# Decode attention and FFN on one core: joint operations for the last three tokens, some paired K loads, and a new order of the work

## The chip, the core and the metric

The kernel runs on one core of a Trainium2 chip. The metric is the device time in microseconds (us) of one execution; before the change its median is 295.55 us in 3 runs (294.45 to 295.8). The engines are PE (matrix multiply; PEld is its weight load), DVE (vector), ACT (scalar functions), POOL (GpSimd) and SP, which here only issues loads and stores to the 16 DMA engines.

## What is computed

Two layers, each an attention step on a cached window and a SwiGLU FFN, for one new position of four sequences (called tokens here):

```python
x = x + A(layernorm(x));  x = x + B(layernorm(x))      # layer 0
x = x + A(layernorm(x));  x = x + B(layernorm(x))      # layer 1: same weights, same caches
# A: B=4, Sq=1, D=448, 16 query heads, 8 K/V heads, Dh=256, window of the last 2048 positions
q = x @ wq; p = softmax(q @ k.T * Dh**-0.5); o = p @ v; return o @ wo
# B: F=1792
return (silu(x @ w_gate) * (x @ w_up)) @ w_down
```

All data are bf16 in memory. One K or V of a token and a head is 1 MB (2048 x 256), and there are 32 of each.

## The kernel before

**Pairs.** The unit of work is a pair of a token and a K/V head in one layer; there are 2 x 32. K and V come in halves of 512 KB, in a pool of 27 slots `half`. For five of the eight heads (`KEEP_K`, `KEEP_V`) the turned K and the V stay in the pool from layer 0 to layer 1, so 44 pairs are loaded and 20 are not. A pair runs through: loads (L852, L872); a DVE turn of each K half into another slot (L858); POOL spreads the query (L875); PE scores, 16 matmuls for each half (L885, with L889); maximum and mask on DVE and PE (L899 to L910); exp on ACT (L913); fold and weights (L918, L921); sums (L927, L930); PV in two halves, either with 512 columns moving (L950) or with V as weights (L943, the last pairs). Then the result is scaled (POOL power L978 or DVE reciprocal L975, L982 to L1001) and projected with `wo` (L1015), accumulated in PSUM bank A. PE gives a K slot back after the scores and a V slot after PV, and SP waits for that before it issues a load into the slot.

**Tokens.** When the eight heads of a token in a layer are done come residual (L740), norm (L560 to L609: sums on DVE, totals over partitions on PE L579, subtraction L583, spread L586, variance L591 to L593, power on POOL L605), FFN (gate and up L693, tanh on ACT L706, products L709 to L717, down L729) and, after layer 0, the next norm and the q projection in three parts (L639 to L661) of two, two and four heads. Pairs of token t-1 in layer 1 alternate with pairs of token t in layer 0. Token 0 is stored on its way; tokens 1 to 3 end together: residual and norm for each (with the two multipliers L608 and L609 on POOL), then one FFN for three in two halves of the columns, written as rows with the residual added through an identity (L761, L777), copied (L784) and stored (L786).

**What sets the order.** The program lists all operations with their dependences, an estimated duration and a rank: the pair's position plus an offset for its kind in three phases (`RANK`) plus a correction for single operations (`TWEAK`). `schedule` walks through time with these estimates and lets each engine take the ready operation of lowest rank; the result is a fixed instruction order for each engine, SP among them. It also hands out the pool's slots: a load takes the slot that has been free longest while more than `RESERVE` are free, and turns use one more spare slot. On the chip each engine runs its list in order and waits on semaphores.

Of the kernel before, what the change touches and what calls it, by code (L numbers as in the profile page):

```python
# [13 lines left out]
B = 4  # L14
# [35 lines left out]
STAY = 0.3  # L50
PAT = 4
ENTER = 0
# [9 lines left out]
RESERVE = 1  # L62
ISSUE = 0.45
LAND = 0.9
DSTART = 2.7
PAGE, PAGE0 = 128, 85
FETCH = 2.65
BUMP = 1.3
# [12 lines left out]
    "exp": (1, 1, 3),  # L81
    "flip": (2, -2, 1.5),
    "fold": (-1, -3, -1.5),
    "high": (-3, -3, -3),
    "inv": (0.6, -0.3, 0),
    "load_k": (0.6, 0, -0.3),
    "load_v": (-0.6, 0, 1),
    "low": (3, -0.3, 1.5),
    "mask": (0, -1, -0.3),
    "max": (0.6, 1, -0.6),  # L90
    "most": (-1, -1.5, 0),
    "neg": (0.3, -0.6, 0),
    "proj": (-1.5, 3, 0.6),
    "pv": (0.3, 1, 0),
    "q": (2, -1.5, -1.5),
    "q_last": (2, 2, 2),
    "scale": (-1.5, 1, -1),
    "scores": (-1, 1.5, 3),
    "spread": (-1, -1, -1),
    "sum": (0.3, -1.5, 3),  # L100
    "sums": (-3, -2, 0),
    "turn": (0.6, 3, -1.5),
    "turn_s": (-3, -3, -3),
    "weights": (2, 1, 1.5),
# [34 lines left out]
class Op:  # L139
# [3 lines left out]
    def __init__(self, i, eng, dur, rank, emit):  # L143
        self.i, self.eng, self.dur, self.rank, self.emit = i, eng, dur, rank, emit
        self.deps = {}
        self.succ = []
        self.nbytes = 0
        self.dsem = None
        self.dval = 0
        self.cell = None  # L150
        self.rel = ()
        self.swap = None
        self.mm = 0
        self.drain = 0.0
        self.inc = False
        self.val = 0
        self.waits = []


class Graph:  # L160
# [56 lines left out]
    def schedule(self, npool):  # L217
# [22 lines left out]
        while n < len(self.ops):  # L240
            best = None
            for e, lst in avail.items():
                if not lst:
                    continue
# [891 lines left out]
```

## Time and profile before

| | |
|---|---|
| median of the runs | 295.55 us |
| the profiled execution | 293.74 us |
| its span, first to last instruction | 291.6 us |
| read from HBM | 104.44 MB |
| share of the span busy: PE, DVE, POOL, ACT | 77%, 74%, 21%, 20% |
| K halves, V halves loaded | 88, 88, of 512 KB |

Times are from the span's start. A row of a group has line, engine, operation, output<-inputs, shapes and xcount, then busy us and mean ns of one. A row of the waits has who waited, for whom, and the total us, number and longest. A row of instructions in time has start, us, engine, line. A stretch of the span has start:end, length, busy us and count of PE, PEld, DVE, ACT and POOL, the granted clock of PE, the DMA engines' busy share and GB/s.

### The profile page before, as it was taken

To read this page: it belongs to the slowest core of one execution; us is meant where nothing else is said; L and a number is where in the kernel's file an instruction comes from. 1 tells how busy PE (TensorE), PEld (TensorE's weight loads), DVE (VectorE), ACT (ScalarE), POOL (GpSimd) and SP (SyncE) were. 2 spreads that over 40 slices of the span, in tenths; PEclk is the share of its full clock that TensorE was granted. 3 is DMA by queue.
4 is the path that set the end of the run, shared out by engine and by line. 5 is a ranking of instruction groups with operands and counts; after the bars stand their busy time and mean duration, and the time that the engine had idled before them with its cause. 6 is when DMAs were issued, how large, how long until landed. Compare 5 with 4: busy or idle time off the path is not lost.

```text
span 291.6 us, 11945 instructions
## 1 busy us (share of the span) xinstructions
PE 223.2 (77%) x5262; PEld 158.1 (54%) x5262; DVE 216.8 (74%) x759; ACT 57.5 (20%) x173; POOL 62.2 (21%) x137
## 2 busy tenths in 40 slices
PE   0544665556649998878896998697989879899984
PEld 0432433334528654656673645574855559675873
DVE  8597556666328979988767988875988997769762
ACT  1002112211001231221112322121123120033311
POOL 1312111111102322221220522022132211142130
PEclk9999999999999999999999999999996555555555
DMA  6999999999999999999999999999899999999400
GB/s 265 393 401 406 405 403 403 402 404 405 387 410 388 405 407 406 410 375 376 398 340 405 410 406 407 364 376 374 297 390 416 407 405 329 290 353 406 198 2 3
DMA packets 31076, 105.20 MB, mean 361 GB/s; under 512 B 3117, under 2 KB 7218, under 8 KB 30642
## 3 DMA queue, kind: packets, MB, share of 16 engines
q1 hardware_dynamic: 31018, 104.45, 92.9%
q8 instruction: 41, 0.67, 0.9%
q14 instruction: 9, 0.07, 0.1%
q10 hardware_dynamic: 8, 0.00, 0.0%
HBM read 104.44 MB, written 0.00 MB: 358 GB/s over the span
## 4 chain that ended last, share of the span: by engine, by line
PE 40%; DMA 27%; DVE 14%; SPq 12%; issue 4%; ACT 1%; POOL 1%; DVEq 0%
DMA half<-in_A_k_cache_dram 24%; PE S L885 11%; PE Y L950 11%; DVE half L858 8%; SPq L872 6%; SPq L852 4%; PE A L1015 3%; PE Z L693 3%; PE Z L639 3%; DMA half<-in_A_v_cache_dram 3%; SPq L537 2%; PE Z L729 2%; PE S L902 2%; PE S L889 2%; PE Y L943 1%
## 5 line engine op out<-in xcount | busy, mean ns | idle before, releaser
L858 DVE STREAM_TRANSPOSE half<-half 128x1024 uint32<-128x1024 uint32 x88 | 108.4, 1232 | 9.5 <-DMA half<-in_A_k_cache_dram 8.8
L885 PE MATMUL S<-qe,half 128*128 128x8 bf16 x2048 | 71.2, 169 | 24.0 <-DVE half L858 14.0
L885 PEld LDWEIGHTS S<-qe,half 128*128 128x128 bf16 x2048 | 64.6, 105 | 33.6 <-DVE half L858 19.1
L950 PE MATMUL Y<-half,pT 128*16 128x512 bf16 x440 | 58.5, 602 | 2.0 <-DMA half<-in_A_v_cache_dram 0.8
L913 ACT ACTIVATE praw<-S,small 128x128 bf16<-128x128 f32 x64 | 23.5, 368 | 136.8 <-DVE S L907 117.0
L978 POOL TENSOR_TENSOR small<-small,expo 128x4 f32<-128x4 f32 (+1 forms) x33 | 29.9, 907 | 65.8 <-DVE small L930 59.8
L875 POOL TENSOR_TENSOR qe<-qc,qmask 128x64 bf16<-128x64 bf16 x64 | 18.7, 292 | 99.6 <-PE S L889 64.7
L982 ACT ACTIVATE oha<-Y 128x512 bf16<-128x512 f32 x33 | 19.6, 595 | 30.0 <-PE Y L950 29.8
L984 DVE SCALAR_TENSOR_TENSOR oha<-oha,small,Y 128x512 bf16<-128x512 bf16 x33 | 24.0, 727 | 1.5 <-ACT oha L982 1.4
L1015 PE MATMUL A<-oT,wo_sb 128*128 128x1 bf16 (+1 forms) x640 | 23.5, 167 | 1.7 <-DVE oT L1001 1.4
L1015 PEld LDWEIGHTS A<-oT,wo_sb 128*128 128x128 bf16 x640 | 21.8, 106 | 4.0 <-DVE oT L1001 2.3
L921 ACT ACTIVATE pT<-S 128x64 bf16<-128x64 f32 x64 | 14.3, 223 | 40.6 <-PE S L918 40.5
L905 DVE STREAM_TRANSPOSE S<-S 128x32 f32<-128x32 f32 x64 | 13.8, 217 | 10.6 <-PE S L902 10.0
L899 DVE TRANSPOSE_TENSOR_REDUCE pmax<-S 128x1 bf16<-128x32 f32 x64 | 13.4, 210 | 11.0 <-PE S L889 8.8
L605 POOL TENSOR_TENSOR st<-st,expo 128x1 f32<-128x1 f32 x16 | 9.0, 561 | 55.7 <-DVE st L593 46.5
L902 PE MATMUL S<-identb,pmax 128*128 128x128 bf16 x64 | 17.8, 278 | 1.6 <-DVE pmax L899 1.4
L907 DVE TENSOR_TENSOR S<-S,amask 128x128 f32<-128x128 f32 x64 | 18.4, 291 | 0.1
L639 PE MATMUL Z<-xn,wq_sb 128*128 128x1 bf16 (+1 forms) x480 | 15.2, 166 | 3.1 <-issue 2.7
L639 PEld LDWEIGHTS Z<-xn,wq_sb 128*128 128x128 bf16 x480 | 14.1, 104 | 5.9 <-issue 2.8
L889 PE MATMUL S<-pbig,identb 128*128 128x128 bf16 x64 | 17.1, 267 | 0.0
L910 DVE TENSOR_REDUCE small<-S 128x1 f32<-128x128 f32 x64 | 16.5, 259 | 0.0
L950 PEld LDWEIGHTS Y<-half,pT 128*16 128x16 bf16 x440 | 8.8, 91 | 13.2 <-DMA half<-in_A_v_cache_dram 5.6
(124 smaller groups left out, 232.4 us busy)
## 6 DMA issues: line engine op xcount, KB each, us to landing
half<-in_A_k_cache_dram SPq DMA_DIRECT2D x88, 512.0 KB, 8.2
half<-in_A_v_cache_dram SPq DMA_DIRECT2D x88, 512.0 KB, 7.7
wo_sb<-in_A_wo_dram SPq DMA_DIRECT2D x8, 448.0 KB, 14.4
wq_sb<-in_A_wq_dram SPq DMA_DIRECT2D x3, 1024.0 KB, 6.9
wd_sb<-in_B_w_down_dram SPq DMA_DIRECT2D x1, 1568.0 KB, 16.6
wg_sb<-in_B_w_gate_dram SPq DMA_DIRECT2D x1, 1344.0 KB, 17.5
wu_sb<-in_B_w_up_dram SPq DMA_DIRECT2D x1, 1344.0 KB, 16.0
wq_sb<-in_A_wq_dram SPq DMA_DIRECT2D x1, 512.0 KB, 10.4
```

The source lines that it names most:

```text
L639: last = e.matmul(o, lhsT=cols(cc, h, ee), rhs=rhs, start=(cc == 0 and hh == 0 and ee == 0), stop=(cc == 3), skip_group_check=True)
L858: return e.transpose(dst[:, :, k0:k1, :], src[:, :, k0:k1, :])
L875: g.op(POOL, 0.25, rk("spread", pos - SLEAD - 1), lambda e: e.tensor_tensor(qe[q_][:, :, :, :], qc[t][:, kvh, :, :].unsqueeze(2).broadcast ...
L885: last = e.matmul(Sb[s_][:, 16 * hf + 8 * gg:16 * hf + 8 * gg + 8], lhsT=kt[:, gg, ce // 2, ce % 2, :], rhs=qe[q_][:, ce, :, :], start=(hf ...
L889: last = e.matmul(Sb[s_][:, 128:256], lhsT=identb[:, :], rhs=pbig[:, :].unsqueeze(1).broadcast_to([128, 64, 2]), start=True, stop=False, s ...
L902: g.op(PE, 0.06, rk("most", pos), lambda e: e.matmul(Sb[s_][:, 128:256], lhsT=pmax[s_][:, 0:1].broadcast_to([128, 128]), rhs=identb[:, :], ...
L913: g.op(SCA, 0.28, rk("exp", pos), lambda e: e.activation(praw[pos % NP][:, :], sM[s_][:, :, :].rearrange("p a r -> p (a r)"), ACT.Exp, bia ...
L950: last = e.matmul(Yb[p_][32 * gg:32 * gg + 16, :], lhsT=pT[mi][:, u:u + 2, :, :, :].rearrange("p u m y n -> p (u m y n)"), rhs=half[vs[hv] ...
L978: g.op(POOL, 0.4 + 0.27 * nm, rk("inv", pos), lambda e: e.tensor_tensor(ri[r_][:, 0:2 * nm], rs[r_][:, 0:2 * nm], expo[:, 1:1 + 2 * nm], o ...
L982: g.op(SCA, 0.48, rk("high", pos), lambda e: e.activation(oh[p_][:, :], Yb[p_][:, :], ACT.Copy), r=(f"y{p_}",), w=(f"oh{p_}",), bank=by)
L984: g.op(DVE, 0.63, rk("low", pos), lambda e: e.scalar_tensor_tensor(out=oh[p_][:, :], in0=oh[p_][:, :], scalar=lomask[:, 0:1], in1=Yb[p_][: ...
L1015: last = e.matmul(Av[:, cc, sl], lhsT=wo_sb[:, 4 * kvh + k, c0:c0 + 128], rhs=oT[ok][:, k % 2, k // 2, 0:n], start=False, stop=False, skip ...
```

## The change

*Last three tokens.* `residuals` and `norms` do for tokens 1 to 3 together, after the last projection, what `residual` and `norm` did for each; the sums are a product and a reduction in place of one operation with an accumulator. One power on POOL serves all three, and the multipliers 0.5r and 0.5r^2 of it are gone: in the FFN of these tokens gate and up are first multiplied by r (the power) on DVE, then one tanh with an immediate scale and two products follow for each half.

```diff
+        def norms(ts, rank, z):
...
+            vec(rank, lambda e: e.tensor_tensor(S_[:, :, 2:6], X, wrow[:, :].unsqueeze(1).broadcast_to([128, n, 4]), op=ALU.mult),
+            vec(rank, lambda e: e.tensor_reduce(S_[:, :, 0:1], S_[:, :, 2:6], AX.X, ALU.add), kw, kv, 0.09)
+            vec(rank, lambda e: e.tensor_tensor(S_[:, :, 2:6], S_[:, :, 2:6], X, op=ALU.mult), kx + kw, kw, 0.08)
+            vec(rank, lambda e: e.tensor_reduce(S_[:, :, 1:2], S_[:, :, 2:6], AX.X, ALU.add), kw, kv, 0.09)
...
+            g.op(POOL, 0.4 + 0.135 * n, rank, lambda e: e.tensor_tensor(
+                S_[:, :, 8:9], S_[:, :, 9:10], expo[:, 0:1].unsqueeze(1).broadcast_to([128, n, 1]), op=ALU.pow), r=kh + ("expo",), w=kr)
...
+                if rows:
...
+                    vec(rank, lambda e, js=js, zg=zg, of=of: e.tensor_tensor(sub(gsf, js), sub(zg[:, 0:gw], js), of(8), op=ALU.mult),
+                    g.op(SCA, 0.2, rank, lambda e, js=js: e.activation(pair_(th_[:, 0:gw], js), pair_(gsf, js), ACT.Tanh, scale=0.5),
...
-                residual(t, pos, layer == 0)
-                norm(t, pos, True, (Sb[(pos_ - 2) % NS], "zs", f"S{(pos_ - 2) % NS}") if (t, layer) == (B - 1, 1) else None)
+                if layer == 0 or t not in ends:
+                    residual(t, pos, layer == 0)
+                    norm(t, pos, True)
+                elif t == B - 1:
+                    assert all(done[(u, 1)] == HKV for u in ends)
+                    residuals(ends, pos)
+                    norms(ends, pos, (Sb[(pos_ - 2) % NS], "zs", f"S{(pos_ - 2) % NS}"))
```

*Pool and loads.* The pool is one tensor; two neighbouring slots that are free at the same time can take both halves of a K in one transfer of 8 KB per partition (seven of the 44 loaded K do, all early). Turns take their slot from the same pool, with `RESERVE` 2. The down weights come in three transfers, two of them with rows of 1792 B in place of 896; for that, neighbouring columns of gate and up are computed in turns (a weight read with a step of two).

```diff
-RESERVE = 1
+RESERVE = 2
...
-            load(rank_d, 1605632, wd_sb[:, :, :], B_w_down.rearrange("(c p) n -> p c n", p=128), "wd", 896)
+            for i, run, gs in ((2, 1792, (0,)), (2, 1792, (1,)), (1, 896, (0, 1))):
...
+                n = 4096 if o.fused == 1 else 2048
+                return e.dma_start(pool[:, 2048 * slot:2048 * slot + n], v[:, 2048 * hf:2048 * hf + n])
...
+                return w[:, c0 + 256 * (f // 2):c0 + 256 * (f // 2) + 256].rearrange("p (m i) -> p i m", i=2)[:, f % 2, :]
```

*Order.* `RANK`, `TWEAK`, the estimated durations and constants of `schedule` are new, so the order changes on every engine. Of the tables two lines:

```diff
-    "scores": (-1, 1.5, 3),
+    "scores": (3, 2, 2),
```

On SP, before, the last loads ahead of the FFN weights and these weights in one block (`half` is the pool):

```order
L872 DMA half<-in_A_v_cache_dram 128x2048 x2
L852 DMA half<-in_A_k_cache_dram 128x2048 x2
L537 DMA wg_sb<-in_B_w_gate_dram 128x3x1792
L537 DMA wg_sb<-in_B_w_gate_dram 128x896
L537 DMA wu_sb<-in_B_w_up_dram 128x3x1792
L537 DMA wu_sb<-in_B_w_up_dram 128x896
L537 DMA wd_sb<-in_B_w_down_dram 128x14x448
L872 DMA half<-in_A_v_cache_dram 128x2048 x2
```

On SP, now, the same place:

```order
L582 DMA wg_sb<-in_B_w_gate_dram 128x896
L582 DMA wo_sb<-in_A_wo_dram 128x2x896 x2
L964 DMA pool<-in_A_k_cache_dram 128x4096
L964 DMA pool<-in_A_v_cache_dram 128x2048
L582 DMA wo_sb<-in_A_wo_dram 128x2x896 x2
L964 DMA pool<-in_A_k_cache_dram 128x2048
L964 DMA pool<-in_A_v_cache_dram 128x2048 x3
L582 DMA wg_sb<-in_B_w_gate_dram 128x3x1792
L582 DMA wu_sb<-in_B_w_up_dram 128x3x1792
L582 DMA wu_sb<-in_B_w_up_dram 128x896
L582 DMA wd_sb<-in_B_w_down_dram 128x3x896
L964 DMA pool<-in_A_v_cache_dram 128x2048 x2
```

and near the program's start, where the small piece of the down weights and paired loads (128x4096) stand:

```order
L964 DMA pool<-in_A_k_cache_dram 128x4096 x2
L964 DMA pool<-in_A_k_cache_dram 128x2048
L964 DMA pool<-in_A_v_cache_dram 128x2048
L964 DMA pool<-in_A_k_cache_dram 128x4096
L964 DMA pool<-in_A_k_cache_dram 128x2048
L582 DMA wd_sb<-in_B_w_down_dram 128x2x448
L582 DMA wo_sb<-in_A_wo_dram 128x2x896
```

The down weights' middle piece stands at the place between. Up to the last FFN weight there are 21 K halves, 16 V halves and all of `wo` before, and 20, 16 and all of `wo` now.

On PE, before, the last projections (`oT`, `oTx`) around the last PV (L943 x32):

```order
L943 MATMUL Y<-pT,half 128x2 x32
L918 MATMUL S<-fold,praw 128x32
L1015 MATMUL A<-oT,wo_sb 128x1 x16
L1015 MATMUL A<-oTx,wo_sb 128x2 x16
L927 MATMUL S<-pT,onesb 128x32
L1015 MATMUL A<-oTx,wo_sb 128x3 x16
L943 MATMUL Y<-pT,half 128x2 x32
L579 MATMUL Z<-st,onesb 128x2 x3
L1015 MATMUL A<-oT,wo_sb 128x1 x16
```

On PE, now, the same place (PV is L1069, the projection L1141):

```order
L1141 MATMUL A<-oT,wo_sb 128x1 x16
L1044 MATMUL S<-fold,praw 128x32
L1141 MATMUL A<-oT,wo_sb 128x1 x16
L1141 MATMUL A<-oTx,wo_sb 128x2 x16
L1053 MATMUL S<-pT,onesb 128x32
L1069 MATMUL Y<-pT,pool 128x2 x32
L1141 MATMUL A<-oTx,wo_sb 128x3 x16
L1141 MATMUL A<-oT,wo_sb 128x1 x16
```

The three-column projection has moved behind the last PV. On DVE, before, what follows the residual of the third token (second row), up to its variance:

```order
L583 TENSOR_SCALAR xn<-xs,Z 128x4
L740 TENSOR_TENSOR xs<-xs,A 128x4
L591 TENSOR_SCALAR st<-Z 128x1
L748 CAST hT<-xs 128x12
L593 TENSOR_SCALAR st<-Z,st 128x1
L601 CAST xe<-Z 128x2
L749 TENSOR_TENSOR hT<-xs,hT 128x12
L566 SCALAR_TENSOR_TENSOR st<-xs,small 128x4
L569 SCALAR_TENSOR_TENSOR st<-st,xs 128x4
L583 TENSOR_SCALAR xn<-xs,Z 128x4
L573 TENSOR_TENSOR st<-st 128x2 x2
L591 TENSOR_SCALAR st<-Z 128x1
```

On DVE, now, from the joint residual (first row) to the subtraction of the mean:

```order
L861 TENSOR_TENSOR xs<-xs,A 128x12
L616 TENSOR_TENSOR st<-xs,small 128x3x4
L867 CAST hT<-xs 128x12
L618 TENSOR_REDUCE st<-st 128x3
L868 TENSOR_TENSOR hT<-xs,hT 128x12
L619 TENSOR_TENSOR st<-st,xs 128x3x4
L620 TENSOR_REDUCE st<-st 128x3
L622 TENSOR_TENSOR st<-st 128x3x2 x2
L631 COPY st<-S 128x3x2
L632 TENSOR_TENSOR xn<-xs,st 128x3x4
```

The rows of the single tokens are gone from behind the last projection, and each step is one row on three columns. On PE, before, after the first token's FFN, from the second part of its q (the L657) to the third (L639 x48; L885 is scores):

```order
L657 MATMUL Z<-qS,rep 128x4x2x4
L902 MATMUL S<-identb,pmax 128x128
L991 MATMUL Y<-osel,oha 128x4 x4
L885 MATMUL S<-qe,half 128x8 x32
L889 MATMUL S<-pbig,identb 128x128
L1015 MATMUL A<-oT,wo_sb 128x1 x16
L639 MATMUL Z<-xn,wq_sb 128x1 x48
L639 MATMUL Z<-xe,wq_sb 128x2 x8
```

On PE, now, the rows just ahead of that third part (L728 x48; L1011 is scores, L1076 PV):

```order
L1011 MATMUL S<-qe,pool 128x8 x16
L1028 MATMUL S<-identb,pmax 128x128
L1011 MATMUL S<-qe,pool 128x8 x16
L1015 MATMUL S<-pbig,identb 128x128
L1076 MATMUL Y<-pool,pT 16x512 x4
L1011 MATMUL S<-qe,pool 128x8 x16
L1015 MATMUL S<-pbig,identb 128x128
L1141 MATMUL A<-oT,wo_sb 128x1 x16
L1044 MATMUL S<-fold,praw 128x32
L1028 MATMUL S<-identb,pmax 128x128 x2
L1076 MATMUL Y<-pool,pT 16x512 x4
L728 MATMUL Z<-xn,wq_sb 128x1 x48
```

The third part has moved behind four more scored halves: 28 are scored when it starts, where 24 were; for the third token 88, where 82 were. The first pair that needs it holds halves 31 and 32 for the first token. In all, PE has 5262 matmuls before and 5252 now; when gate and up of the last token in layer 0 start, 108 of the 128 halves are scored before, 109 now.

More of the change, by code (lines that the diff above doesn't have):

```diff
@@ L80 @@
 RANK = {
[L81 to L97, printed above, removed]
-    "scores": (-1, 1.5, 3),
[L99 to L104, printed above, removed]
+    "exp": (-0.6, 3, 2),
+    "flip": (3, 2, 1),
+    "fold": (-0.3, -0.3, -0.3),
+    "inv": (3, 1.5, 1.5),
+    "load_v": (0, 0, 0.3),
+    "low": (0.6, -2, 0),
+    "mask": (2, -0.6, -0.3),
+    "max": (-0.6, -0.6, -0.6),
+    "most": (0, -0.3, 0),
+    "neg": (2, 1.5, 1.5),
+    "proj": (-0.3, -0.3, -0.3),
+    "pv": (3, 3, 0.3),
+    "q": (2, 2, 2),
+    "q_last": (-0.6, 2, -3),
+    "scale": (2, 2, -2),
+    "scores": (3, 2, 2),
+    "spread": (3, 1.5, 3),
+    "sum": (-1, -1, 0),
+    "sums": (-1, -1, -1),
+    "turn": (1, 1, 1),
+    "turn_s": (-0.3, -2, -1.5),
+    "weights": (1, 1, 1),
 }
 TWEAK = {
[17 rows of a table removed]
[17 rows of a table added]
 }
@@ L250, in schedule @@
                             continue
+                        t0 = t
                         t = max(t, min(pool)[0])
+                        w = o.mate
+                        if w is not None and w.i > o.i and not o.fused and not w.fused:
+                            pr = two(t0) if len(pool) > RESERVE + 1 else None
+                            if pr and pr[0] <= t + FUSEW:
+                                t = pr[0]
+                            else:
+                                pr = None
+                                t += FUSEW
                 else:
@@ L314, in schedule @@
                 pool.append((o.end + TAIL[o.eng], c[0], o))
-            for s in o.succ:
+            if o.fused == 1:
+                w = o.mate
+                avail[e].remove(w)
+                w.start, w.end, w.dsem, w.dval, w.pos = t, o.end, o.dsem, o.dval, len(order[e])
+                order[e].append(w)
+                n += 1
+            for s in o.succ + (o.mate.succ if o.fused == 1 else []):
                 left[s] -= 1
-                if o.eng == SP and not s.deps[o]:
+                if o.eng == SP and not s.deps.get(o, True):
                     ready_at[s] = max(ready_at[s], o.start + o.dur)
@@ L414, in build @@
         wd_sb = sb("wd_sb", [128, NFC, D], BF16)
[L415 removed]
+        pool = sb("pool", [128, 8 * DH * NPOOL], BF16)
+        half = [pool[:, 8 * DH * i:8 * DH * i + 8 * DH] for i in range(NPOOL)]
         identb = sb("identb", [128, 128], BF16)
```

193 lines of the change are left out of this document (142 added, 51 removed), and 34 rows, old and new, of the table TWEAK.

## The prediction

> **What bounds the kernel now.** I read the page's head first, then the DMA rows by stretches of the span, then what the load queue and the engines wait for, and last the instructions of the final 17 us in order of time.
>
> ```profile
> span 291.6 us, 11945 instructions
> ...
> PE 223.2 (77%) x5262; PEld 158.1 (54%) x5262; DVE 216.8 (74%) x759; ACT 57.5 (20%) x173; POOL 62.2 (21%) x137
> ...
> GB/s 265 393 401 406 405 403 403 402 404 405 387 410 388 405 407 406 410 375 376 398 340 405 410 406 407 364 376 374 297 390 416 407 405 329 290 353 406 198 2 3
> ```
>
> No engine is busy all the time, while GB/s (a value per 7.3 us) stands near 405 for half of the span, sags in the other half and is nothing in the last two slices. The next rows give the same in stretches; the last two columns are the busy share of the DMA engines and GB/s.
>
> ```profile
> 6.00:10.00 4.00, 1.16 (x13) 0.75 (x13) 2.95 (x32) 0.00 (x0) 1.12 (x2) 1.00 1.01 426
> 24.00:66.00 42.00, 24.84 (x415) 14.57 (x415) 26.69 (x61) 6.98 (x21) 7.33 (x14) 1.00 1.03 403
> 72.00:84.00 12.00, 5.51 (x160) 4.90 (x161) 3.91 (x22) 0.64 (x2) 1.19 (x4) 1.00 1.05 395
> 84.00:126.00 42.00, 37.51 (x865) 25.09 (x862) 35.48 (x107) 9.51 (x29) 10.01 (x21) 1.00 1.02 403
> 126.00:216.00 90.00, 77.83 (x1874) 55.08 (x1875) 72.28 (x247) 19.95 (x62) 20.99 (x44) 1.00 1.00 378
> 216.00:273.00 57.00, 51.69 (x1242) 37.12 (x1239) 47.28 (x157) 14.30 (x44) 14.31 (x28) 0.55 0.99 375
> 273.00:276.00 3.00, 3.00 (x108) 3.00 (x106) 1.54 (x8) 0.86 (x4) 0.00 (x0) 0.50 0.13 51
> ```
>
> Three stages are to be seen. Up to 126 us the DMA runs at 403 GB/s and PE and DVE have room: **bytes bound it**. From 126 to 273 us it runs at 378 and 375. What is missing there is 90 x (1 - 378/403) + 57 x (1 - 375/403) = 5.6 + 4.0 = **9.5 us of DMA time**, the most that a better order could win in this stage. At about 273.5 us the last load has landed, and the 18 us behind it are a chain of small instructions.
>
> ```profile
> SPq L852 <- PE Y L950: 22.4, 17, 5.0
> ...
> SPq L872 <- PE S L885: 23.6, 11, 4.4
> ...
> PE Z L729 <- DMA wd_sb<-in_B_w_down_dram: 3.3, 1, 3.3
> ```
>
> The two SPq rows (total, times, longest) say why the DMA starves: the load queue holds K and V loads back until PE has finished with a slot of the pool. Most of such waits cost nothing because loads are queued ahead; 9.5 us is what came through. The third row is FFN work at 80 us that waited for the down weights.
>
> ```profile
> 277.47 0.22 ACT L921 ACTIVATE pT<-S 128x64 bf16<-128x64 f32 x1 [0.37 <-PE S L918]
> ...
> 278.15 0.57 PE L1015 MATMUL A<-oTx,wo_sb 128*128 128x3 bf16 x16
> ...
> 278.57 0.99 PE L943 MATMUL Y<-pT,half 128*128 128x2 bf16 x32
> ...
> 279.95 0.56 PE L1015 MATMUL A<-oT,wo_sb 128*128 128x1 bf16 x16
> ...
> 280.56 0.16 DVE L740 TENSOR_TENSOR xs<-xs,A 128x4 f32<-128x4 f32 x1 [0.19 <-PE A L1015]
> ...
> 281.22 0.16 DVE L566 SCALAR_TENSOR_TENSOR st<-xs,small 128x4 f32<-128x4 f32 x1
> ...
> 281.42 0.16 DVE L569 SCALAR_TENSOR_TENSOR st<-st,xs 128x4 f32<-128x4 f32 x1
> ...
> 282.14 0.24 PE L579 MATMUL S<-st,onesb 128*128 128x2 bf16 x3
> ...
> 282.53 0.23 DVE L583 TENSOR_SCALAR xn<-xs,S 128x4 bf16<-128x4 f32 x1
> ...
> 282.89 0.78 PE L693 MATMUL Z<-xn,wg_sb 128*128 128x3 bf16 x24
> ...
> 283.63 0.57 POOL L605 TENSOR_TENSOR st<-st,expo 128x1 f32<-128x1 f32 x1
> ...
> 284.69 0.27 ACT L706 ACTIVATE qS<-Z,st 128x8 f32<-128x8 f32 x1 [0.30 <-POOL st L608]
> ...
> 285.42 0.22 PE L693 MATMUL S<-xe,wu_sb 128*128 128x6 bf16 x3
> ...
> 285.97 0.87 ACT L706 ACTIVATE qS<-S,st 128x6 f32<-128x6 f32 x3 [1.00 <-DVE qS L717]
> ...
> 285.99 0.92 PE L777 MATMUL A<-wd_sb,qS 128*3 128x112 bf16 x32 [0.34 <-DVE qS L717]
> ...
> 287.85 0.73 PE L777 MATMUL A<-wd_sb,qS 128*3 128x112 bf16 x24 [0.94 <-DVE qS L717]
> 288.63 0.28 DVE L784 CAST oha<-A 128x112 bf16<-128x112 f32 x1 [0.83 <-PE A L777]
> ```
>
> This is the tail (start, duration): last PV, last output projection, residual, norm of the third token, gate and up, three powers on POOL, tanh, products, down, copy. PE is done with gate and up at 285.64, but down starts at 285.99 and its second part only at 287.85: the powers and the ACT and DVE work per token set the end.
>
> **The change part by part.**
>
> *The last PV.* The weights for it are written at 277.47 + 0.22 = 277.69, yet PE runs three groups of 16 projections first. The last of them (3 columns) starts at 278.15 and the PV at 278.57. In the new order that group stands behind the PV, where PE waits for DVE anyway: **-0.4 us**, so the last projection goes from 279.95 to 279.55 and the residual from 280.56 to 280.15.
>
> *Residual and norm of three tokens together.* Before, two tokens were done under the last projection and only the third was exposed: 282.89 - 280.56 = 2.33 us from its residual to the first gate matmul. Now all three wait for the last projection, but in one instruction per step. A dependent step costs 281.42 - 281.22 = 0.20. The residual, five arithmetic steps and the two subtractions that follow one another take 6 x 0.20 + 0.18 = 1.38; totals and their way back 282.53 - 282.14 = 0.39 and 0.05 before; the new copy of the totals 0.20; from the subtraction to the first gate matmul 282.89 - 282.53 = 0.36. Sum 2.38, so 0.05 longer: what is given up by waiting is what was hidden, and it costs nothing more. Gate starts at 282.5.
>
> *Gate and up, then down.* 98 matmuls from 282.89 to 285.42 + 0.22, so 2.75 us; now to 285.3. The weights are read with a step of two columns; the q projection does that already, and its weight load takes 104 ns, as the gate's does:
>
> ```profile
> L978 POOL TENSOR_TENSOR small<-small,expo 128x4 f32<-128x4 f32 (+1 forms) x33 | 29.9, 907 | 65.8 <-DVE small L930 59.8
> ...
> L605 POOL TENSOR_TENSOR st<-st,expo 128x1 f32<-128x1 f32 x16 | 9.0, 561 | 55.7 <-DVE st L593 46.5
> ...
> L907 DVE TENSOR_TENSOR S<-S,amask 128x128 f32<-128x128 f32 x64 | 18.4, 291 | 0.1
> ...
> L639 PEld LDWEIGHTS Z<-xn,wq_sb 128*128 128x128 bf16 x480 | 14.1, 104 | 5.9 <-issue 2.8
> ```
>
> Down needs 0.78 for its 24 matmuls up to the copy; the 32 take 0.92 with the same 0.28 of latency in it, so 0.02 each, and all 56 in one piece 0.78 + 0.64 = 1.42. If the products are there in time, the copy starts at 285.3 + 0.05 + 1.42 = 286.8.
>
> *Are they in time?* One power for three columns: 561 ns for one column and 907 for four (rows above) are the bounds, 0.79 on the line between them. It starts after copy, subtraction, square and sum (four steps of 0.20 from 281.95), at 282.75, and ends at 283.55, where before the third of three ended at 284.20. Then scale, tanh (0.27), two products and the up scaling: 1.2 us for the first half, and 1.15 for the second behind it on DVE: 285.9. Down's second part can start at 285.3 + 0.64 = 285.95. The two chains end together, so neither has slack. Copy 288.63 to 286.8: **the tail gives -1.9 us with the 0.4 in it**. If joint steps cost 0.05 more each (the row of 3 x 4 elements doesn't exist, L907's 0.29 does) it is -1.3; with a faster power -2.2.
>
> *Loads of 8 KB runs and the down weights in three pieces.* Seven of the 44 K pairs become one transfer, all before the gate weights. At 8 KB runs the trace has only the q weights: 426 GB/s (6 to 10 us) against 403. 7 x 1.05 MB at 403 is 18.2 us, at 426 17.2: -1.0, all in the stage that bytes bound; the ends are 0 and -1.0. [...] Before the last byte of the down weights there are now 36 K and V halves instead of 37, so it lands 0.52 MB / 403 = 1.3 us earlier, and the 3.3 us wait shrinks by about 1.1, since gate and up land 0.4 MB later. A fused pair delivers its first half 1.3 us later; the cover is that DVE is busy 27 of 42 us there. How much of these 2.1 us reaches the end isn't in the trace: nothing, if the pool is as full at 126 us as now; all, if the 9.5 us shrink by it. I take **-0.9**.
>
> *Slots and new ranks.* The pool still keeps two slots back (before one kept plus one spare). PE's work is the same to 10 matmuls of 5262, and when the FFN of the last token begins, 109 halves are scored instead of 108. Nothing in the trace prices the rest of the new order; its bounds are -9.5 (all starvation gone) and the +5.2 worked out below. I take 0, the nearest to what the equal counts say.
>
> **Sum**: -1.9 - 0.9 = -2.8. The profiled execution took 293.74 us (span 291.6), so 290.9. It lies 1.8 below the median of the runs, 295.55; against that the forecast is **292.7 us**.
>
> **The rivals.**
>
> *Slower: the third part of a q projection comes late.* The 56 matmuls of heads 2, 3, 6 and 7 now stand behind four more scored halves for the first token (28 instead of 24) and six more for the third (88 instead of 82); the first pair that needs them is two halves on. PE works in order: if q isn't there, scores and every PV behind them stop, slots stay taken and the DMA starves.
>
> ```profile
> 203.77 1.37 PE Z L639 x48
> ...
> L858 DVE STREAM_TRANSPOSE half<-half 128x1024 uint32<-128x1024 uint32 x88 | 108.4, 1232 | 9.5 <-DMA half<-in_A_k_cache_dram 8.8
> ...
> L875 POOL TENSOR_TENSOR qe<-qc,qmask 128x64 bf16<-128x64 bf16 x64 | 18.7, 292 | 99.6 <-PE S L889 64.7
> ```
>
> 48 matmuls take 1.37, 56 so 1.6; two DVE steps, one matmul and the spread (292 ns) add about 1.0 at 0.2 to 0.3 each. Uncovered that is 2.6 us per token, 5.2 for both: 292.7 + 5.2 = **297.9**. It decides from the point where the two halves in between (0.9 us of PE work) are scored before the spread ends. For it: the gap is 2 halves where it was 6. Against: DVE has two more halves to turn in that gap, 2 x 1.23 us, nearly the whole 2.6.
>
> *No change:* the same at one of the two tokens only: -2.8 + 2.6, so **295.4**.
>
> *Much faster:* the new order also ends half of the starvation: 292.7 - 4.75 = **288.0**. For it: the starvation comes in lumps around the FFN and q stretches, where the order matters most. Against: the counts at those places hardly move.
>
> *The array's clock.*
>
> ```profile
> L950 PE MATMUL Y<-half,pT x440: 379/596/634, 24.1 to 271.1; 128*16 128x512 bf16 x147
> ...
> 214.16 1.88 PE L950 MATMUL Y<-half,pT 128*16 128x512 bf16 x16
> ...
> 219.93 0.82 PE L950 MATMUL Y<-half,pT 128*16 128x512 bf16 x12 [0.31 <-ACT pT L921]
> ```
>
> Groups of four 512-column matmuls follow each other by 0.43 us at 214 (1.88 for four groups) but by 0.22 at 219.9 (0.82 for three), and single ones take 379 or about 600 ns. So for some 3 us PE ran at twice the rate, and nearly nowhere else: the granted clock of 1.00 ahead of 221 us is not to be read as speed. If the new order keeps that state, 110 groups save 0.21 each, 23 us of PE, of which the DMA lets 9.5 through: 295.55 - 1.9 - 9.5 = **284.2**. [...]
>
> **How the numbers follow.** Forecast 0.38 (own range 291.3 to 294.0), much faster 0.17, clock 0.03, no change 0.15, slower 0.27. A measurement can tell about 0.5%, 1.5 us, from no change; so faster 0.58, same 0.15, slower 0.27. The range goes from the much faster case to the slower one, 287.8 to 298.2, and leaves out the clock, losses beyond one chain for each token, and gains of over half of the starvation.
>
> **What would show it.** Tail: from the end of the last projection to the copy of the output 6.7 us instead of 8.1, one power of about 0.8 us, down in one piece. Loads: the FFN's wait for down weights under 2.5 us. Order: GB/s from 126 us to the last load still near 377; under 370 with PE waiting for the spread of q would be the slower rival, over 390 the faster one. Wrong would be the tail if PE waits over 0.3 us between up and down, or if gate starts more than 2.7 us after the residual.

## The result and the profile after

The changed kernel takes **293.03 us** (median of 22 runs, 290.87 to 295.95) against 295.38 us of the kernel before beside it (22 runs, 292.71 to 299.07): ratio **0.9937, 95% interval 0.991 to 0.9965**, so 1.9 us less (0.9 to 2.7). Two more timings in the study gave 0.9979 (0.9948 to 1.001) and 0.995 (0.9909 to 0.9992). Weighted by their intervals the three give 0.9954 with 0.0018 to either side: 1.4 us less, give or take 0.5. Forecast were 2.8. The ratios leave out the slowest executions of either kernel, so they are not quite the ratio of the medians.

The page's head after, to be held against the three rows of before:

```profile
span 291.1 us, 11884 instructions
...
PE 224.1 (77%) x5252; PEld 159.2 (55%) x5252; DVE 215.5 (74%) x736; ACT 55.6 (19%) x169; POOL 59.8 (21%) x129
...
GB/s 260 422 407 404 412 409 403 404 400 407 396 409 409 408 407 405 401 383 359 410 307 414 410 406 393 359 366 339 355 413 409 382 380 401 304 283 386 225 5 3
```

The shares of the engines hardly move. In the stretches (same columns as before) the gain at the front and the starvation behind it can be told apart:

```profile
12.00:18.00 6.00, 4.22 (x120) 3.56 (x118) 4.04 (x16) 0.00 (x0) 0.89 (x3) 1.00 1.01 419
...
24.00:66.00 42.00, 23.38 (x424) 14.05 (x425) 27.87 (x63) 7.21 (x21) 6.52 (x14) 1.00 1.03 406
72.00:84.00 12.00, 7.95 (x213) 6.35 (x209) 4.59 (x29) 1.35 (x4) 2.35 (x5) 1.00 1.03 401
84.00:126.00 42.00, 37.73 (x835) 25.68 (x832) 36.65 (x99) 10.41 (x32) 10.11 (x21) 1.00 1.03 406
126.00:216.00 90.00, 79.60 (x1880) 56.24 (x1876) 71.97 (x249) 18.56 (x59) 20.87 (x44) 1.00 0.99 377
216.00:273.00 57.00, 50.39 (x1204) 36.39 (x1208) 44.94 (x149) 13.05 (x41) 13.19 (x27) 1.00 0.97 368
273.00:276.00 3.00, 3.00 (x88) 2.29 (x80) 2.43 (x12) 1.08 (x3) 1.01 (x1) 1.00 0.13 49
```

The paired loads run at 419 GB/s between 12 and 18 us. From 126 us on 377 and 368 stand where 378 and 375 stood; the missing DMA time is 90 x (1 - 377/403) + 57 x (1 - 368/403) = 5.8 + 5.0 = 10.8 us instead of 9.5. The loads end at the same time: the rate falls near 273.5 us (49 GB/s in the last stretch, 51 before), and the last packet of K and V, which comes later than the forecast read it, lands at 274.90 us (275.33 before). So in these two executions **almost nothing of the head's gain is left when the last load lands**, and the rest is decided behind it. Single executions spread more than that: in the two later ones of the changed kernel the last packet lands at 273.68 and at 276.28. The final instructions in order of time:

```profile
279.02 0.22 ACT L1047 ACTIVATE pT<-S 128x64 bf16<-128x64 f32 x1 [0.90 <-PE S L1044]
...
279.70 1.00 PE L1069 MATMUL Y<-pT,pool 128*128 128x2 bf16 x32
...
280.56 0.57 PE L1141 MATMUL A<-oTx,wo_sb 128*128 128x3 bf16 x16
...
280.99 0.56 PE L1141 MATMUL A<-oT,wo_sb 128*128 128x1 bf16 x16
281.59 0.17 DVE L861 TENSOR_TENSOR xs<-xs,A 128x12 f32<-128x12 f32 x1 [0.69 <-PE A L1141]
...
283.83 0.78 PE L788 MATMUL Z<-xn,wg_sb 128*128 128x3 bf16 x24
...
284.04 0.85 POOL L646 TENSOR_TENSOR st<-st,expo 128x3 f32<-128x3 f32 x1 [9.47 <-DVE st L642]
...
286.37 0.22 PE L788 MATMUL S<-xe,wu_sb 128*128 128x6 bf16 x3
...
286.52 1.48 PE L896 MATMUL A<-wd_sb,qS 128*3 128x112 bf16 x56
...
286.89 0.18 DVE L815 SCALAR_TENSOR_TENSOR qS<-qS 128x18 bf16<-128x18 f32 x1
288.05 0.28 DVE L903 CAST oha<-A 128x112 bf16<-128x112 f32 x1 [0.97 <-PE A L896]
```

From the last weights (279.02 + 0.22) to the copy are 8.81 us, before 288.63 - 277.69 = 10.94: **the tail is 2.13 us shorter**. But the last weights themselves come 1.55 us later than before, at the same last landing.

### The profile page after: what moved, and what is told of

It reads as the page before. It is cut to its first block, busy times and chain, and to the rows that moved or that the text cites. A ratio compares the mean times of both kernels' runs of the same rounds, so it can differ in the third digit from the quotient of the medians.

```text
span 291.1 us, 11884 instructions
## 1 busy us (share of the span) xinstructions
PE 224.1 (77%) x5252; PEld 159.2 (55%) x5252; DVE 215.5 (74%) x736; ACT 55.6 (19%) x169; POOL 59.8 (21%) x129
## 4 chain that ended last, share of the span: by engine, by line
PE 52%; DVE 16%; DMA 15%; SPq 9%; issue 5%; ACT 1%
DMA pool<-in_A_k_cache_dram 15%; PE S L1011 15%; PE Y L1076 12%; DVE pool L981 9%; SPq L964 6%; PE A L1141 5%; PE Z L728 4%; PE Z L788 3%; SPq L582 3%; PE S L1015 2%; PE S L1028 2%; PE Y L1069 2%; PE Z L843 2%; DVE oha L1110 1%; DVE S L1033 1%
## 5 line engine op out<-in xcount | busy, mean ns | idle before, releaser
L981 DVE STREAM_TRANSPOSE pool<-pool 128x1024 uint32<-128x1024 uint32 x88 | 107.9, 1231 | 7.0 <-DMA pool<-in_A_k_cache_dram 4.6
L1011 PE MATMUL S<-qe,pool 128*128 128x8 bf16 x2048 | 70.9, 169 | 24.2 <-DVE pool L981 18.3
L1011 PEld LDWEIGHTS S<-qe,pool 128*128 128x128 bf16 x2048 | 64.3, 105 | 35.1 <-DVE pool L981 22.2
L1076 PE MATMUL Y<-pool,pT 128*16 128x512 bf16 x440 | 60.5, 609 | 0.3 <-DMA pool<-in_A_v_cache_dram 0.3
L1141 PE MATMUL A<-oT,wo_sb 128*128 128x1 bf16 (+1 forms) x640 | 23.1, 167 | 1.5 <-issue 0.8
L1141 PEld LDWEIGHTS A<-oT,wo_sb 128*128 128x128 bf16 x640 | 21.1, 105 | 4.3 <-issue 2.3
L1076 PEld LDWEIGHTS Y<-pool,pT 128*16 128x16 bf16 x440 | 10.2, 94 | 12.6 <-issue 5.4
L1044 PE MATMUL S<-fold,praw 128*128 128x32 bf16 x64 | 13.0, 204 | 4.0 <-ACT praw L1039 3.8
L728 PEld LDWEIGHTS Z<-xn,wq_sb 128*128 128x128 bf16 x480 | 14.0, 104 | 2.1 <-DVE st L680 0.4
L728 PE MATMUL Z<-xn,wq_sb 128*128 128x1 bf16 (+1 forms) x480 | 14.9, 166 | 0.2 <-DVE xn L672 0.2
```

Of the source, the lines that this page charges most:

```text
L728: last = e.matmul(o, lhsT=cols(cc, h, ee), rhs=rhs, start=(cc == 0 and hh == 0 and ee == 0), stop=(cc == 3), skip_group_check=True)
L981: return e.transpose(dst[:, :, k0:k1, :], src[:, :, k0:k1, :])
L1011: last = e.matmul(Sb[s_][:, 16 * hf + 8 * gg:16 * hf + 8 * gg + 8], lhsT=kt[:, gg, ce // 2, ce % 2, :], rhs=qe[q_][:, ce, :, :], start=(hf ...
L1076: last = e.matmul(Yb[p_][32 * gg:32 * gg + 16, :], lhsT=pT[mi][:, u:u + 2, :, :, :].rearrange("p u m y n -> p (u m y n)"), rhs=half[vs[hv] ...
L1141: last = e.matmul(Av[:, cc, sl], lhsT=wo_sb[:, 4 * kvh + k, c0:c0 + 128], rhs=oT[ok][:, k % 2, k // 2, 0:n], start=False, stop=False, skip ...
```

## The experiments

A ratio is always that to the kernel before on the same chip, with its 95% interval; "last pT" is the end of the last write of the weights, and "tail" the time from there to the copy of the output, both from one profiled execution.

**Joint tail alone, in the kernel before.** The body's order stays as it was up to the last pair.

```diff
+        def residuals(ts, rank):
+        def norms(ts, rank, z):
...
-                residual(t, pos, layer == 0)
-                norm(t, pos, True, (Sb[(pos_ - 2) % NS], "zs", f"S{(pos_ - 2) % NS}") if (t, layer) == (B - 1, 1) else None)
+                if layer == 0 or t not in ends:
+                    residual(t, pos, layer == 0)
+                    norm(t, pos, True)
+                elif t == B - 1:
+                    residuals(ends, pos)
+                    norms(ends, pos, (Sb[(pos_ - 2) % NS], "zs", f"S{(pos_ - 2) % NS}"))
...
-            g.op(PE, 16 * MM, rk("proj", pos), emit,
+            g.op(PE, 16 * MM, rk("proj", pos) + 100 * (n == 3), emit,
```

> The kernel before with the joint tail alone: residual, norm, tanh and products of the last three tokens together, and the three-column projection behind the last PV; every instruction up to the last pair stands as before, on every engine. Theory: the tail is all of the gain, so the time from the weights of the last PV to the copy of the output falls from 10.94 to about 8.8 us and the whole is 2.1 us faster than before, ratio 0.993, equal to the changed kernel within 0.8 us. Rival (the loads and the new order matter as well, by the 0.9 us forecast for them): 2.1 faster than before but 0.9 slower than the changed kernel or more. Second rival (the new order loses, and the loads win it back): faster than the changed kernel by over 0.8 us.

Measured 0.9969 (0.9926 to 1.0011), 293.16 us; tail 9.33. As expected, the three-column projection stands behind the last PV here too, but it took 0.85 us instead of 0.57 in this execution, and gate of both halves runs ahead of up (from the last projection's end to the copy 6.74 instead of 6.50): so the tail gains 1.61 and not 2.13. By runs it is 0.9 us (loss of 0.3 to gain of 2.2), which holds that figure.

**Separate tail, in the changed kernel.** The opposite: residual, norm, tanh and products for each token as before, all else as changed.

```diff
-                elif t == B - 1:
-                    residuals(ends, pos)
-                    norms(ends, pos, (Sb[(pos_ - 2) % NS], "zs", f"S{(pos_ - 2) % NS}"))
+                residual(t, pos, layer == 0)
+                norm(t, pos, True, (Sb[(pos_ - 2) % NS], "zs", f"S{(pos_ - 2) % NS}") if (t, layer) == (B - 1, 1) else None)
```

> The changed kernel with the old tail: residual and norm for each token, three tanh and three scalings for each half, three-column projection ahead of the last PV; loads and order up to the last pair as in the changed kernel. Theory: 2.1 to 2.6 us slower than the changed kernel, so at the time of the kernel before, within 0.8 us. Rival (loads and new order gain 0.9): 0.9 faster than before. Second rival (the new order loses): slower than before by over 0.8.

Measured 1.0081 (1.0042 to 1.012), 296.63 us; tail 10.96, that of before to 0.02. This is the second rival of the expectation: **with the old tail the changed kernel is slower than the kernel before**, though its pairs and earlier down weights are in place. The joint tail is worth 1.0081 - 0.9954 = 1.27% here (0.43% to either side, 3.7 us), and 0.31% (0.42%) in the other body. Together that is 0.79% or 2.3 us (0.9 to either side), and the traces say 2.13 for the same instructions. That the two differ by more than their intervals allow isn't explained.

**Pairs as two loads each.** The seven pairs of K halves are issued as two transfers of 4 KB runs, back to back.

```diff
-                return e.dma_start(pool[:, 2048 * slot:2048 * slot + n], v[:, 2048 * hf:2048 * hf + n])
+                h = [e.dma_start(pool[:, 2048 * (slot + i):2048 * (slot + i) + 2048], v[:, 2048 * (hf + i):2048 * (hf + i) + 2048])
+                     for i in range(2 if o.fused == 1 else 1)]
```

> The changed kernel with each of the seven paired K loads issued as two of 4 KB runs, at the same place in the queue. Theory: the first 126 us lose up to 1.0 us of DMA time (406 GB/s falls to 403 or so in the stretches of the head), and nothing of it reaches the end: within 0.7 us of the changed kernel. Rival: the 1.0 us is passed on, 0.7 to 1.0 us slower. [...]

Measured 0.9996 (0.9963 to 1.0029), 293.54 us. The stretch in which the changed kernel moves 419 GB/s:

```profile
12.00:18.00 6.00, 4.22 (x120) 3.56 (x118) 4.05 (x16) 0.00 (x0) 0.91 (x3) 1.00 1.02 401
```

It is 401 here. Against 0.9954 the pairs are worth 0.42% (0.38% to either side), 1.2 us: the rival of the expectation, not its theory, though only just clear of nothing.

**Gate weights loaded twice.** 1.376 MB more are read early, ahead of the FFN, into the place where they belong; at 403 GB/s that is 3.4 us of the load queue.

```diff
+            if kvh == first[0][0]:
+                g.dose_at = len(g.ops)
...
+        g.dose = lambda e: e.dma_start(wg_sb[:, 0:3 * FF].rearrange("p (c n) -> p c n", c=3),
+                                       B_w_gate[0:384, :].rearrange("(c p) n -> p c n", p=128))
```

> The changed kernel with the gate weights (1.376 MB) loaded a second time, early, ahead of the first wo load: 1.376 MB / 403 = 3.4 us more DMA time in the stage that bytes bound, nothing else changed. Theory (the stage behind 126 us has its own bound, slots and engines, so the head has slack): the first FFN's down matmuls start 3.4 us later, starvation after 126 us shrinks by about as much, and the end moves by less than 1.2 us. Rival (bytes of the head are passed on to the end): 2.5 to 3.4 us slower.

Measured 1.0059 (1.0024 to 1.0094), 296.04 us: against 0.9954 it costs 1.05%, 3.1 us (1.2 to either side). My theory that the head has slack fell. **Here 3.4 us of added bytes in the early queue came to about 3.1 us at the end.** That the time which the pairs save there counts as well follows by argument; the runs with and without pairs agree with it, just clear of nothing.

**Four kernels beside each other: the changed one again, old ranks, down weights, last pair.** The first is unaltered:

> The changed kernel itself, unaltered, so that the three kernels beside it are compared on one chip. Both theories: 0.994 of the kernel before, as its 22 runs gave (0.991 to 0.9965), so about 1.9 us below it. What it can tell: the two kernels with separate tail (1.0081) and joint tail (0.9937) were not timed beside each other, and their difference of 4.2 us is twice the 2.1 us that the traces show from the last pT to the copy. If this run comes out near 0.999 (1.8 us more), the joint tail is worth what its trace says; if it stays at 0.994, the rest of the 4.2 us has yet to be found.

It gave 0.9979 (0.9948 to 1.001), 293.4 us, and a tail of 8.80. Of the three timings of this kernel the first is the most favourable.

*Old ranks under the new slot rule:* `RANK`, `TWEAK`, the estimated durations and the constants of the planner are those of before, the tail joint, the loads paired (seven pairs, not five as I expected).

```diff
-STAY = 0
+STAY = 0.3
-ENTER = 0.09
+ENTER = 0
...
-    "scores": (3, 2, 2),
+    "scores": (-1, 1.5, 3),
```

> The changed kernel with the rank table, the single ranks and the planner's constants of before: joint tail, five pairs in 8 KB runs at the start, down weights in three pieces behind the up weights as before. Theory, that the new ranks give back part of what tail and loads gain: the trace of the changed kernel loses 1.3 us of transfers between 126 and 273 us and 1.5 us between the last landing and the last pT against that of before; with the old ranks both stay away, so the sum is the tail's -2.1 and up to -0.7 from five pairs (5 times 0.14 us), 2.1 to 2.8 us below before, ratio 0.9905 to 0.993, transfers from 126 to 273 us at 377 GB/s, last pT 3.5 to 4.5 us after the last landing. Rival, that ranks are neutral and the body's difference is the spread of runs: the same as the changed kernel, ratio 0.994 to 0.995. A second rival: the planner places the old ranks' instructions over another allocation of slots, and its own model ends 13 us later than for the new ranks; if the model is right in sign, the kernel is slower than before, ratio above 1.005.

Measured **1.0298** (1.0229 to 1.0368), 302.85 us. The second rival holds: ranks and slot rule can't be taken apart. What this kernel has beside the old order, above all the new rule of handing out slots, costs some 12 us under the old ranks (8.8 measured, and the 3 that tail and pairs should gain on top); the new ranks bring 10 of it back (1.0298 to 0.9954). The old ranks had been made for the old rule; which part of the rule costs it was not tried.

*Down weights last:* the two pieces that the changed kernel loads early are put behind the third.

```diff
-    106: -2.5, 110: -3.5, 111: -8.5, 112: 1.5,
+    106: -2.5, 112: 1.5,
```

> The changed kernel with the two pieces of the down weights that it loads early (0.92 MB) put back behind the third, so that 1.6 MB of down weights lie behind the up weights as before; the number of bytes and runs and nearly all else of the order are unchanged. Theory, that only the time of bytes in the queue counts: the wait of the first down projection grows from 1.2 us to about 3.3 us, and the end moves by less than 0.5 us (ratio to the changed kernel 1.000). Rival, the prediction's second term of the loads taken at its bound: the first projections 1.1 to 2.2 us later are passed on, ratio to the changed kernel 1.004 to 1.0075.

Measured 0.9982 (0.9947 to 1.0017) beside the 0.9979, with medians of 293.34 and 293.40 us. The means of the two differ by 0.1 us with 0.8 to either side, which hardly leaves room for the 1.1 us that the rival asked at least. The waits of TensorE for the down weights, in the changed kernel

```profile
PE Z L843 <- DMA wd_sb<-in_B_w_down_dram: 1.2, 1, 1.2
```

and in this one

```profile
PE Z L842 <- DMA wd_sb<-in_B_w_down_dram: 2.6, 1, 2.6
```

show that the first down projection does start later, and that the end doesn't notice. The theory holds; the prediction's second term of the loads isn't borne out.

*Last pair first:* nine single ranks (1743 stood at -2.3, the others at 0), so that the last pair's scores and fold stand ahead of projections of earlier pairs.

```diff
+    1652: 4.3, 1653: 4.3, 1717: -10, 1742: -6, 1743: -6.3, 1752: 4, 1754: 3.5, 1755: 3.5, 1688: 3.5,
```

> The changed kernel with ten single ranks altered, all of instructions of the last three pairs: the last pair's scores ahead of the projections of an earlier pair, its fold ahead of them too, and these projections between fold and the last weighted sum. Theory A, that the 1.5 us more between last landing and last pT are the order of the last pair: its fold then follows the exponential by 0.15 instead of 0.67 us and its scores run about 1 us earlier; last pT 1.0 to 1.5 us earlier, and the end 0.5 to 1.0 us earlier, 0.9965 to 0.998 of the changed kernel. Theory B, that TensorE brings a backlog of work into the last stretch (it is busy in all of 255 to 281 us) and the new order of it only moves the pieces about: last pT earlier, but the last projection within 0.3 us of the changed kernel's place, and the time the same.

Measured 0.9985 (0.9947 to 1.0022). In order of time:

```profile
277.64 0.19 PE L1044 MATMUL S<-fold,praw 128*128 128x32 bf16 x1
...
278.20 0.99 PE L1141 MATMUL A<-oT,wo_sb 128*128 128x1 bf16 x32
279.05 0.56 PE L1141 MATMUL A<-oTx,wo_sb 128*128 128x2 bf16 x16
279.48 0.19 PE L1053 MATMUL S<-pT,onesb 128*128 128x32 bf16 x1
279.50 0.57 PE L1141 MATMUL A<-oTx,wo_sb 128*128 128x3 bf16 x16
279.94 0.99 PE L1069 MATMUL Y<-pT,pool 128*128 128x2 bf16 x32
281.19 0.59 PE L1141 MATMUL A<-oT,wo_sb 128*128 128x1 bf16 x16 [0.26 <-DVE oT L1127]
```

The fold runs about 1.15 us earlier than in the changed kernel's first trace (278.79), the last weights are ready at 278.08, and then the projections that had been put back fill the time: the last projection stands at 281.19, against 280.99. Theory B, a backlog of TensorE work in the last stretch, is what this run shows. This one new order of the end doesn't bring the 1.55 us back; other orders were not tried.

**The parts put on the kernel before, beside the changed kernel.**

> The changed kernel unaltered, to be compared with the three beside it on one chip. 0.9955 of the kernel before, between the 0.994 and the 0.998 of its two earlier timings, so 1.3 us below.

Measured 0.995 (0.9909 to 0.9992), 293.23 us.

*Seven paired K alone:* the load order and the other engines' orders of before are unchanged; slots are renumbered after planning so that the halves lie side by side.

```diff
+    def pair_up(self, npool):
...
+            if w is not None and w.i > o.i and o in fresh and w in fresh:
+                o.fused, w.fused = 1, 2
+                taken[o.cell[0]] = len(taken)
+                taken[w.cell[0]] = len(taken)
```

> The kernel before with seven of its first K pairs as one transfer of 8 KB runs each, the load order and the other engines' order unchanged: only the slots are renumbered so that the halves of these pairs lie side by side. Theory, that time saved in the queue ahead of the FFN is passed on whole: 7 times 0.14 us, 1.0 us below before, ratio 0.9965, and 420 GB/s or so between 12 and 24 us. Rival, that the fuller pool starves the queue later and takes it back: ratio 1.000 to 1.001.

Measured 0.9982 (0.9947 to 1.0017), 293.46 us. Its stretch of paired loads:

```profile
12.00:18.00 6.00, 3.77 (x118) 3.33 (x115) 4.45 (x14) 0.00 (x0) 0.69 (x2) 1.00 1.02 418
```

against this one in the kernel before:

```profile
12.00:18.00 6.00, 3.94 (x124) 3.51 (x123) 4.55 (x16) 0.00 (x0) 0.70 (x2) 1.00 1.01 378
```

That is 418 GB/s for 378, but 387 stood there in the kernel with the joint tail alone, which loads the same, so part of the difference is spread. By itself the run can't tell 1.0 us from nothing; with the 0.42% of the opposite experiment the pairs are worth 0.29% (0.26% to either side), 0.9 us.

*Joint tail and seven pairs, with ranks, slot rule and down weights of before.* To the two edits above comes the order of gate and up that the changed kernel has:

```diff
-                    rank_ = rank + 0.1 * (rows and wk == "wu")
+                    rank_ = rank + 0.1 * (rows and wk == "wu") + 0.3 * pi * bool(rows)
```

> The kernel before with the joint tail in the order that it has in the changed kernel (the three-column projection behind the last weighted sum, gate and up of one half after the other) and the seven pairs, but with its own ranks, slot rule and down weights in one transfer. Theory, that the new ranks and slot rule give back part of the gain: tail -2.1 and pairs -1.0 add up, 3.1 us below before, ratio 0.9895, and 1.0 to 1.8 us below the changed kernel beside it; last pT at 276.5 to 277, copy 8.8 us later. Rival, that ranks and slot rule are neutral: equal to the changed kernel, ratio 0.994 to 0.997.

Measured **0.9919** (0.9875 to 0.9963), 292.57 us; tail 8.81:

```profile
278.17 0.22 ACT L1035 ACTIVATE pT<-S 128x64 bf16<-128x64 f32 x1 [1.89 <-PE S L1032]
...
287.20 0.28 DVE L893 CAST oha<-A 128x112 bf16<-128x112 f32 x1 [0.97 <-PE A L886]
```

The tail is the changed kernel's to 0.01 us, in another body. The last pT, expected at 276.5 to 277, came at 278.39. The sum of 3.1 us lies in the interval (1.1 to 3.7), and the median is 0.7 us under the changed kernel beside it; but 0.9919 and 0.995 overlap, so the rival isn't excluded by this run.

*Five V pairs as well:*

```diff
+                    if hv:
+                        two[0].mate, two[1].mate = two[1], two[0]
```

> The same with five V pairs of the first loads as 8 KB runs as well, twelve pairs in all. By the theory of time in the queue another 5 times 0.14 us: 3.8 us below before, ratio 0.987. By its rival no more than the kernel with seven pairs; a V pair lands its first half 1.3 us later, which matters only if weighted sums wait for it (list of waits).

Measured **0.9925** (0.9885 to 0.9965), 291.99 us (289.51 to 292.9). That is faster than the kernel before by 2.2 us (1.0 to 3.4) with none of the new ranks, and the lowest median of all the kernels here. That it beats the changed kernel is not shown: 0.9925 against 0.9954, with 0.4% and 0.2% to either side. The 0.987 of the theory lies outside the interval, and the V pairs' own 0.7 us don't show.

## Why the forecast was right in sign and too large

The prediction said 292.7 and the first timing gave 293.03; the median of before moved from 295.55 to 295.38, so of the forecast 2.8 us 1.9 came (1.4 in the three timings). That 293.03 lies so near 292.7 is partly luck: it is the most favourable of three timings, and the other two gained 0.6 and 1.5 us by their ratios. By its steps:

*Tail, -1.9 forecast, -2.13 measured.* The three-column projection: the last PV starts 279.70 - 279.24 = 0.46 behind the weights instead of 0.88, so -0.42 for -0.4. Residual to first gate matmul 283.83 - 281.59 = 2.24 for 2.38; the difference lies in the way from the totals to their copy (0.28 for 0.39) and from the subtraction to the gate (0.32 for 0.36). The power 0.85 for 0.79. Gate and up 2.76 for 2.75. Products ready at 287.07, when down's second part could start at 286.52 + 0.64 = 287.16: the tie that was forecast, with 0.09 to spare. From the last projection's end (281.55) to the copy 6.50, forecast 6.7, before 8.12. The runs agree in sign in both directions (joint into before, separate into after), singly with 0.9 and 3.7 us, in the mean with 2.3. This step was right, and it carries the result: without it the changed kernel is slower than the kernel before.

*Loads, -0.9 forecast.* The bound -1.0 of the pairs agrees with the runs (0.9, with 0.8 to either side, and the doubled gate weights, 3.1 us at the end for 3.4 in the queue, show that the early queue passed added bytes on). At the same place of the queue 8 KB runs gave 419 GB/s and 4 KB runs 401. The packets in that stretch of the traces say the same: one of 8192 B takes 309 ns in the median and one of 4096 B 159, so two small ones take 9 ns more than a large one. The bound -1.1 of the down weights isn't borne out: the wait shrank from 3.3 to 1.2 us, by 2.1 where 1.1 was forecast, yet giving 1.4 us of it back changed nothing that the runs can tell. Earlier arrival of the same bytes isn't fewer bytes. The -0.9 was nearly right since it happened to lie between.

*Slots and new ranks, 0 forecast: the step that failed.* Tail and pairs make -3.1, the runs -1.4 (0.5 to either side); so this term is about **+1.7 us**, by subtraction, and known to no better than 1 us either way. Its sign doesn't hang on that sum: the kernel with the separate tail has the new order, the pairs and a tail as long as that of before, and it is 2.4 us slower than the kernel before (1.2 to either side). The direct comparison, tail and pairs on the old order against the changed kernel (0.9919 against 0.9954), gives +1.0 us with 1.4 to either side and by itself leaves 0 open. Five executions with the body of before and five with the new one point the same way and show where the time goes (the last column is the time from the end of the last packet of K and V to last pT, in the same order):

| body | edits | last pT, us | last packet to last pT, us |
|---|---|---|---|
| before | none; joint tail; paired K; both; both with V pairs | 277.69, 277.54, 278.82, 278.39, 277.92 | 2.36, 2.69, 3.96, 3.27, 2.71 |
| new | changed kernel, twice; separate tail; unpaired; down weights last | 279.24, 278.79, 280.48, 280.08, 278.08 | 4.34, 5.11, 6.29, 7.04, 6.32 |

The means of last pT are 278.1 and 279.3, although four of the five new bodies had pairs and only three of the old. No single pair of traces would show it: the two groups overlap, and 12 runs of one program spread over 290.31 to 297.11. (The third execution of the changed kernel, 295.03 us where its timing has a median of 293.23, is not in the table: 281.28 and 5.00.) The last column does not overlap: 3.0 us in the mean with the old body, 5.8 with the new. The last packet itself lands no later with the new body, at 273.5 in the mean against 275.1. So the loss lies **behind the last load**: with the new order more work is left when the data are in. Which work, and why, stays open; the last-pair run had 3.55 us there, but its last projection came no earlier. More starvation is not the place, although the changed kernel's trace has 1.3 us more of it. Worked out as above, the missing DMA time from 126 to 273 us is 9.4 to 9.7 us in the three traces without pairs, and 10.1 to 10.9 in those with pairs on the old body, against 10.8 in the changed kernel and 10.0 to 12.6 in the other traces of the new body with pairs: it comes with the pairs, not with the ranks.

"Nothing" also hid two large pieces: with the old ranks the new slot rule costs some 12 us, and the new ranks recover 10. I had taken 0 as nearest to equal counts of scored halves; equal counts say nothing on slots.

*The rivals.* The late third part of q didn't come: the waits of TensorE after the change name the turned K, never the spread query. They name q's own repeat only in the first 21 us, long before the first of these q projections (96 us):

```profile
PE S L1011 <- DVE pool L981: 18.3, 18, 5.5
...
PE Z L746 <- DVE qc L750: 3.6, 4, 1.2
```

Most of the wait for the turned K also lies early: behind 126 us it is 3.5 us, where 4.1 stood before. The rate over the whole of 126 to 273 us is 373.5 GB/s, between the 377 of the forecast and the 370 named as this rival's sign. Half of the starvation did not end, it grew. The faster array did not come, as the list of one line's instructions shows:

```profile
L1076 PE MATMUL Y<-pool,pT x440: 586/596/635, 31.2 to 273.1; 128*16 128x512 bf16 x147
```

The shortest is 586 ns where 379 stood before.

## What to carry to other kernels

Price a chain of small dependent instructions from its rows: the tail came out within 0.3 us and carried over to another body to 0.01 us. In a kernel whose start is bound by bytes, ask of every early change whether it alters the time in the queue or only brings the same bytes forward; here bytes added to the queue reached the end (1.376 MB cost 3.1 us), and bytes brought forward did not (0.92 MB, with no difference that the runs can tell). A new order of the whole program is not worth "nothing" because counts agree: put the local edits on the old order first, as here, and see what the new order adds to them.

## What the hardware showed beside that

*The granted clock in the profile was no measure of speed here.* From 216 to 273 us it was 0.55 before and 1.00 after, while the 512-column matmuls kept TensorE busy for 15.22 us before (124 of them) and 14.15 after (116): 123 and 122 ns for each.

*TensorE stands still at regular places.* In the changed kernel's trace, and in a second execution of the same program, matmuls start late with nothing that they waited for. The first execution:

```profile
143.80 0.46 PE L1011 MATMUL S<-qe,pool 128*128 128x8 bf16 x12 [1.39 <-issue]
...
251.65 0.29 PE L1028 MATMUL S<-identb,pmax 128*128 128x128 bf16 x1 [2.27 <-issue]
```

The second:

```profile
143.20 0.46 PE L1011 MATMUL S<-qe,pool 128*128 128x8 bf16 x12 [0.57 <-issue]
...
251.17 0.29 PE L1028 MATMUL S<-identb,pmax 128*128 128x128 bf16 x1 [2.27 <-issue]
```

There are eight to ten such stops, 8.2 us in all in each of these two executions and 5.9 in that of before. They don't tell the two orders apart: over all traces with the body of before they come to 5.1 to 8.9 us. Six come at the same instructions in both executions, with lengths that change from run to run (1.39 and 0.57 us at the first). A queue of kind "instruction" with 41 packets, 0.67 MB in all, stands among the DMA queues. Each of the ten stops of the first execution ends 1.2 to 1.6 us after such a packet of 16 KB has ended, and each of the eight in that of before 1.3 to 1.5 us after one, though most of the 41 are followed by no stop. So these packets are a candidate for the cause; that wasn't tried.
